# First token block with gate, value and last output pair in three float32r products, weight splits staged through device memory, and one written-out order

## The chip, the cores and the metric

The kernel runs on one core of one Trainium2 chip. The metric is device time of one execution in microseconds (us), lower is better. The engines named below are TensorE (PE in the profile; PEld is its weight load), VectorE (DVE), ScalarE (ACT), GpSimd (POOL) and SyncE (SP). SP and POOL do no arithmetic here that matters; they issue the DMAs, each in its own program order.

## The reference

Attention without a softmax over scores, then a gated feed-forward layer, all in float32:

```python
def _attn_ref(q, k, v):                      # batch 8, heads 8, seq 576, head_dim 64
    q_s = softmax(q, axis=-1)                # max, exp, sum + 1e-09
    k_s = softmax(k, axis=2)
    kv = np.einsum('bhsd,bhse->bhde', k_s, v)
    return np.einsum('bhsd,bhde->bhse', q_s, kv)

def _moe_ref(x, w_gate, w_val, w_out):       # 4608 tokens, d_model 512, d_ff 1536
    gate = 1.0 / (1.0 + np.exp(-(x @ w_gate)))
    val = x @ w_val
    return gate * val @ w_out
```

`x` is the attention output, tokens by 512 features. The float32 weights come to the chip as pairs of 32-bit words (float64 bits) and are narrowed there.

## The kernel before

The 4608 tokens go in nine token blocks of 512 (`w` = 0 to 8; the change calls a block a span). The 1536 hidden columns go in twelve slices `j` of 128, or six pairs `p` of two slices. For each block the kernel makes `x` (512 features by 512 tokens), then hidden activations by two products (gate and value), a sigmoid, a product, and the output product.

Blocks 1 to 8 work in split float32r: each operand is a high part (float32 rounded to float32r) plus a low part (the rest), and a product is three matmuls, high by high, high by low, low by high, each with 256 columns. Gate and value of a pair are done by a seven-product scheme (`g1`, matmuls on L770) on a 2x2 blocking: three weight blocks A11, A12, A22 stay in memory on the core for good as high and low parts (`a_w`), and four sums of weight blocks, S1 to S4, go through one buffer `s_sb`, which is loaded again for each pair from device memory (`s_load`, L311, 512 KB each). The output product (`g2`, L856) takes `wo_hl`, high and low parts of the output weights, also loaded for each pair (`wo_load`, L261).

Token block 0 is different. It runs while the weights arrive, and its products are plain float32 matmuls of 512 columns: `g1_0` (L718) for gate and value, `g2_0` (L752) for the output, one slice `j` at a time. Each plain float32 matmul stands in the trace as two records. Beside it, in the same 130 us, the weights are prepared for the later blocks: narrowed (`w_low`, `w_top`, `w_join`, the same for `wo`), summed (`w_sums`, into the buffer `four`), split (`split_hi` on ACT L294, `split_lo` on DVE L299; `wo_hi` on ACT L244, `wo_save` on DVE L248), and the high and low parts of the sums and of the output weights are stored to device memory by POOL (L304, L251). The attention part of block 1 runs there too.

Token block 1 goes through the pairs in the order 5, 0, 1, 2, 3, 4, so that the pair split last comes first. The finished block 0 leaves through `acc_out`: four ACT copies from the accumulators into `x_32` (L744), then four DMAs from `x_32` (L745, issued by SP).

The order of work is the order of the calls in the code: on each engine the instructions run in that order, each waiting for what it needs. Where the transposed row maxima of the next block's queries are needed (`qn_send`, `q_spread`), SP sends them to device memory and reads them back spread over partitions (L517, L559), for the maxima and later for the reciprocals. Three PSUM buffers `gv` serve all gate and value products; `y` and `z` of a pair are copied out by ACT (L793 to L812) between products that add to them.

```python
def g1_0(j):            # block 0: 2 x 4 plain float32 matmuls of 512 columns
    nc.tensor.matmul(ps[n], lhsT=w[:, kt // 2, sl], rhs=x_0[:, kt], ...)
```

Of the kernel before, what the change touches and what calls it, by code (L numbers as in the profile page):

```python
# [8 lines left out]
F32 = mybir.dt.float32  # L9
# [8 lines left out]
P = 128  # L18
# [32 lines left out]

@with_exitstack
def attn_moe(ctx: ExitStack, tc: tile.TileContext, qf, qn, qT, k, kT, v, wgv, wo, out):
# [34 lines left out]
    f_last = const.tile([P, 4, 2, 2 * P], F32, name="f_last")  # L88
    s_dram = [spool.tile([P, 4 * 4 * 2 * P], F32, name=f"s_{p}") for p in range(NS)]
# [116 lines left out]
    def w_on_vector(j):  # L206
        return j == 1

    def w_low(j):
        narrow_low(w_raw[j])  # L210
        if w_on_vector(j):
            narrow_sign_bits(w_raw[j])

    def w_top(j):
        if not w_on_vector(j):
            narrow_sign(w_raw[j])
        narrow_abs(w_raw[j], w_both(j))

    def w_join(j):
        narrow_join(w_raw[j], w_both(j))  # L220

    def wo_on_vector(j):
        return j % 2 and j > 6

    def wo_low(j):
        narrow_low(wo_raw[j])
        if wo_on_vector(j):
            narrow_sign_bits(wo_raw[j])

    def wo_top(j):  # L230
        if j % 2 == 0:
            wo_t[j // 2] = wpool.tile([P, 2, DM], F32, name="wo_t")
        if not wo_on_vector(j):
            narrow_sign(wo_raw[j])
        narrow_abs(wo_raw[j], wo_t[j // 2][:, j % 2])
# [28 lines left out]

    s_32 = {}

    def w_sums(p):

        f = f_w[p].rearrange("p b n e -> p b (n e)")
        s_32[p] = t = four  # L270

        def tt(o, x, y, op):
            nc.vector.tensor_tensor(out=t[:, o], in0=x, in1=y, op=op)

        tt(S1, f[:, 2], f[:, 3], ALU.add)
        tt(S2, t[:, S1], f[:, 0], ALU.subtract)
        tt(S3, f[:, 0], f[:, 2], ALU.subtract)
        tt(S4, f[:, 1], t[:, S2], ALU.subtract)

    def split_of(p):  # L280
        f = f_w[p].rearrange("p b n e -> p b (n e)")
        s = s_sb.rearrange("p s h n e -> p s h (n e)")
        a = a_w[p].rearrange("p b h n e -> p b h (n e)")
        return [(a[:, A11:A12 + 1], f[:, 0:2])] + [
            (s[:, i:i + 2], s_32[p][:, i:i + 2]) for i in (0, 2)
        ] + [(a[:, A22:A22 + 1], f[:, 3:4])]

    def split_hi(p, parts=range(4)):

        if p not in a_w:  # L290
            a_w[p] = apool.tile([P, 3, 2, 2, 2 * P], F32R, name="a_w", tag=f"a{p}")
        for i in parts:
            o, x = split_of(p)[i]
            nc.scalar.copy(out=o[:, :, 0], in_=x)  # L294

    def split_lo(p, parts=range(4)):
        for i in parts:
            o, x = split_of(p)[i]
            nc.vector.tensor_tensor(  # L299
                out=o[:, :, 1], in0=x, in1=o[:, :, 0].bitcast(F32), op=ALU.subtract  # L300
            )
            if 1 <= i <= 2:
                n = 8 * 2 * P
# [1038 lines left out]
```

## Time and profile before

| | |
|---|---|
| Device time, median of 3 runs | 926.0 us (924.47 to 926.96) |
| Profiled execution, from its first to its last instruction | 925.1 us |
| PE busy | 917.0 us, 99% |
| DVE busy | 604.7 us, 65% |
| ACT busy | 478.6 us, 52% |
| POOL busy | 168.2 us, 18% |
| DMA, mean over the span | 278 GB/s |
| Granted PE clock | 1.00 |

The page gives no other time for the profiled execution than its span; it lies inside the spread of the three timed runs, 0.9 us below their median. PE is busy nearly all the time, so what PE has to do, and the few places where it stands still, make the time. The share of DVE and ACT is an average: both are far busier while block 0 runs than later.

### The profile page before, as it was taken

How to read it: one execution, taken by the hardware profiler on the slowest of the kernel's cores; microseconds unless marked ns; L12 is line 12 of the kernel's file. 1: busy time of each engine (PE TensorE's matmuls, PEld its weight loads, DVE VectorE, ACT ScalarE, POOL GpSimd, SP SyncE). 2: the span in 40 equal slices, each digit the busy share in tenths (PEclk: the TensorE clock that was granted, in tenths of full speed). 3: DMA queues.
4: the chain of work that ended last, by engine and by line, in shares of the span. 5: the costliest groups of instructions: out<-in, count | busy, mean ns of one | idle time of the engine just before them, and what ended most of it. 6: DMA issues, size and time to landing. Idle time of an engine off the chain costs nothing.

```text
span 925.1 us, 18593 instructions
## 1 busy us (share of the span) xinstructions
PE 917.0 (99%) x7556; PEld 835.5 (90%) x7556; DVE 604.7 (65%) x973; ACT 478.6 (52%) x800; POOL 168.2 (18%) x320
## 2 busy tenths in 40 slices
PE   9999999998999999999999999999999999999998
PEld 6445545898999999999999999999999999999998
DVE  7998979846766577656766666666746574664242
ACT  3879986735455455644663456354725443543222
POOL 0010101221121212122121122112221122212220
PEclk9999999999999999999999999999999999999999
DMA  9995776999899999999999899999997799768772
GB/s 311 390 398 194 288 254 252 361 336 319 214 311 330 323 247 264 325 325 289 236 326 326 285 246 302 323 289 251 304 302 209 224 262 324 232 187 257 214 208 69
DMA packets 93268, 256.93 MB, mean 278 GB/s; under 512 B 15160, under 2 KB 17728, under 8 KB 90240
## 3 DMA queue, kind: packets, MB, share of 16 engines
q0 software_dynamic: 44288, 167.27, 60.4%
q1 hardware_dynamic: 48896, 88.47, 32.4%
q8 instruction: 60, 0.98, 0.4%
q14 instruction: 24, 0.20, 0.1%
HBM read 227.15 MB, written 28.56 MB: 276 GB/s over the span
## 4 chain that ended last, share of the span: by engine, by line
PE 91%; DMA 5%; DVE 1%; SPq 1%; ACT 1%; issue 0%; DVEq 0%
PE gv L770 46%; PE acc L856 27%; PE gv L718 9%; PE acc L752 4%; PE gv L637 2%; PE at L440 2%; DMA four<-q_m_row 2%; DMA out<-x 1%; DMA ring<-qT_in 1%; PE at L637 1%; DMA wo_raw<-wo_in 1%; SPq L396 1%; DMA lent<-k_in 1%; PE acc L658 0%; DVE q_m L525 0%
## 5 line engine op out<-in xcount | busy, mean ns | idle before, releaser
L770 PE MATMUL gv<-c_hl,s_sb 128*128 128x256 f32 x2304 | 277.4, 276 | 2.9 <-ACT sg L802 2.7
L770 PEld LDWEIGHTS gv<-c_hl,s_sb 128*128 128x128 f32 x2304 | 268.7, 188 | 3.5 <-ACT sg L802 3.1
L856 PE MATMUL acc<-wo_hl,h 128*128 128x256 f32 x2304 | 269.4, 276 | 0.0
L856 PEld LDWEIGHTS acc<-wo_hl,h 128*128 128x128 f32 x2304 | 264.6, 188 | 0.4
L770 PE MATMUL gv<-c_hl,a_w 128*128 128x256 f32 x1728 | 220.2, 277 | 0.0
L770 PEld LDWEIGHTS gv<-c_hl,a_w 128*128 128x128 f32 x1728 | 206.9, 188 | 1.0 <-issue 0.7
L311 POOL DMA_DIRECT2D s_sb<-s x188 | 101.3, 539 | 308.5 <-PE gv L770 303.2
L789 DVE TENSOR_TENSOR sg<-gv,sg 128x512 f32<-128x512 f32 x48 | 33.2, 691 | 152.5 <-PE gv L770 152.5
L261 POOL DMA_DIRECT2D wo_hl<-wo x94 | 50.7, 539 | 280.1 <-PE acc L856 280.1
L802 ACT COPY sg<-gv 128x512 f32<-128x512 f32 x48 | 28.2, 587 | 131.4 <-PE gv L770 121.7
L812 ACT COPY sg<-gv 128x512 f32<-128x512 f32 x48 | 28.2, 587 | 99.8 <-PE gv L770 99.8
L814 DVE TENSOR_TENSOR sg<-sg 128x512 f32<-128x512 f32 x48 | 33.2, 692 | 56.8 <-ACT sg L812 56.8
L718 PE MATMUL gv<-x,f_w 128*128 128x512 f32 x160 | 70.2, 593 | 0.0
L718 PEld LDWEIGHTS gv<-x,f_w 128*128 128x128 f32 x160 | 30.0, 190 | 36.3 <-issue 34.2
L835 DVE TENSOR_TENSOR h<-sg,h 128x1024 fp32r<-128x1024 f32 x48 | 58.8, 1226 | 1.6
L817 ACT ACTIVATE sg<-sg 128x512 f32<-128x512 f32 x48 | 30.4, 634 | 50.3 <-DVE sg L816 50.3
L823 DVE TENSOR_TENSOR sg<-sg 128x512 f32<-128x512 f32 x48 | 33.2, 692 | 33.6 <-ACT sg L817 33.6
L798 ACT COPY sg<-gv 128x512 f32<-128x512 f32 x48 | 28.2, 587 | 40.3 <-PE gv L770 40.3
L793 ACT COPY sg<-gv 128x512 f32<-128x512 f32 x48 | 28.2, 587 | 36.2 <-PE gv L770 36.2
L752 PE MATMUL acc<-wo_t,h 128*128 128x512 f32 x96 | 43.2, 592 | 0.0
L752 PEld LDWEIGHTS acc<-wo_t,h 128*128 128x128 f32 x96 | 18.2, 190 | 22.5 <-issue 21.8
L816 DVE TENSOR_TENSOR sg<-gv,sg 128x512 f32<-128x512 f32 x48 | 33.2, 691 | 2.7 <-PE gv L770 0.5
(162 smaller groups left out, 993.6 us busy)
## 6 DMA issues: line engine op xcount, KB each, us to landing
s_sb<-s POOLq DMA_DIRECT2D x188, 512.0 KB, 7.3
wo_hl<-wo POOLq DMA_DIRECT2D x94, 512.0 KB, 6.1
s<-s_sb POOLq DMA_DIRECT2D x12, 1024.0 KB, 6.6
out<-x SPq DMA_DIRECT2D x35, 256.0 KB, 5.5
ring<-k_in SPq DMA_DIRECT2D x28, 256.0 KB, 6.0
ring<-qn_in SPq DMA_DIRECT2D x28, 256.0 KB, 4.8
four<-q_m_row SPq DMA_DIRECT2D x56, 128.0 KB, 12.0
ring<-qT_in SPq DMA_DIRECT2D x28, 256.0 KB, 10.4
```

Of the source, the lines that this page charges most:

```text
L261: nc.gpsimd.dma_start(out=t.rearrange("p h e -> p (h e)"), in_=wo_dram[2 * p + i].bitcast(F32R))
L311: nc.gpsimd.dma_start(out=s_sb[:, i].rearrange("p h n e -> p (h n e)"), in_=s_dram[p][:, i * n:(i + 1) * n].bitcast(F32R),)
L718: nc.tensor.matmul(ps[n], lhsT=w[:, kt // 2, sl], rhs=x_0[:, kt], start=(kt == 0), stop=(kt == NK - 1),)
L752: nc.tensor.matmul(acc[0][m], lhsT=h_0[j][:, m * P:(m + 1) * P], rhs=wo_t[j // 2][:, j % 2], start=(j == 0), stop=(j == NJ - 1),)
L770: nc.tensor.matmul(ps[:, n], lhsT=lh(kt), rhs=c_hl[i][:, x, kt], start=(first and n == 0 and kt == 0 and lh is wh and x == 0), stop=(last ...
L789: nc.vector.tensor_tensor(out=sg[:, 0], in0=rr, in1=sg[:, 0], op=ALU.add)
L814: nc.vector.tensor_tensor(out=sg[:, 3], in0=sg[:, 3], in1=sg[:, 2], op=ALU.add)
L816: nc.vector.tensor_tensor(out=sg[:, 1], in0=z, in1=sg[:, 1], op=ALU.add)
L817: nc.scalar.activation(sg[:, 0:2, 0], sg[:, 0:2, 0], AF.Sigmoid)
L823: tt(out=sg[:, 0:2, 0], in0=sg[:, 0:2, 0], in1=sg[:, 0:2, 1], op=ALU.mult)
L835: nc.vector.tensor_tensor(out=lo, in0=sg[:, :, 0], in1=hi.bitcast(F32), op=ALU.subtract)
L856: nc.tensor.matmul(acc[w][m][:, es], lhsT=h[lh][:, i, sl], rhs=o[i][:, rh, es], start=(at == 0 and i == 0 and lh == 0 and rh == 0 and e == 0),
```

## The change

Block 0 takes split operands for gate and value. Its `x` is split on the way out of the accumulators (`x_hi` on ACT, `x_lo` on DVE), and slices `j` are multiplied as three products from the high and low parts of A11, A12, A22 and, new, A21, whose parts lie in half of `s_sb` for the time. The output product stays plain float32 for slices 0 to 9 and is split for 10 and 11.

The sums S1 to S4 and the output weights of pairs 0 to 4 are no longer split in block 0. They are stored as float32 (`s_save`, `wo_save`; 1 MB and 512 KB a pair), and in block 1, pair by pair, read back into a staging buffer (`s_in` into the four slots of `x_32`, `wo_in` into part of `f_last`, 256 KB each), split there (`s_hi`, `wo_hi` on ACT; `s_lo`, `wo_lo` on DVE) into `s_sb` and `wo_hl`, used, and stored as high and low parts (`s_store`, `wo_store`, 512 KB each) for blocks 2 to 8. Block 1 so loads no high and low parts.

From the first instruction to the end of block 1, one written list of some 1,000 words gives the order (`ORDER`, played by `go`); blocks 2 to 8 keep their loops.

```diff
+ORDER = """
+k0_in.0 warm.16 k0_in.2 k0_in.4 warm.2 q0_in.0.2 q0_in.2.2 k_own.0 v_load.0.3 load_w.0 k_top.1
...
+g2_0.10 c_hi.6 g_mul_0.11 s_in.0.2 g1_s2.5 s_hi.0.1 h_hi_0.11 g1_s1.5 s_lo.0.1 h_lo_0.11
...
-    def wo_save(j):
-        t = wo_out[j]
-        nc.vector.tensor_tensor(
-            out=t[:, 1], in0=wo_t[j // 2][:, j % 2], in1=t[:, 0].bitcast(F32), op=ALU.subtract
-        )
-        nc.gpsimd.dma_start(out=wo_dram[j], in_=t.rearrange("p h e -> p (h e)").bitcast(F32))
+    def wo_save(p):
+        nc.gpsimd.dma_start(out=wo32_dram[p], in_=wo_t[p].rearrange("p h e -> p (h e)"))
...
+    def s_save(p):
+        t = four
+        if p < NS - 1:
+            nc.gpsimd.dma_start(
+                out=s32_dram[p], in_=t.rearrange("p s e -> p (s e)")
+            )
...
+        if j % 2 == 0:
+            return [(a_w[p][:, A11:A12 + 1], f[:, 0:2])]
+        if p not in t21:
+            t21[p] = s_sb[:, p % 2:p % 2 + 1]
+        return [(t21[p], f[:, 2:3]), (a_w[p][:, A22:A22 + 1], f[:, 3:4])]
...
+    def stage(i):
+        return x_32[:, i] if i < 4 else f_last[:, 3].rearrange("p n e -> p (n e)")
...
+    def s_in(p, i, eng=nc.sync):
+        n = 2 * 2 * P
+        eng.dma_start(out=stage(i), in_=s32_dram[p][:, i * n:(i + 1) * n])
+
+    def s_hi(p, i):
+        nc.scalar.copy(out=s_sb[:, i, 0].rearrange("p n e -> p (n e)"), in_=s_src(p, i))
+
+    def s_lo(p, i):
+        hi, lo = (s_sb[:, i, h].rearrange("p n e -> p (n e)") for h in range(2))
+        nc.vector.tensor_tensor(out=lo, in0=s_src(p, i), in1=hi.bitcast(F32), op=ALU.subtract)
+
+    def s_store(p, i):
+        n = 4 * 2 * P
+        nc.gpsimd.dma_start(
+            out=s_dram[p][:, i * n:(i + 1) * n],
+            in_=s_sb[:, i].rearrange("p h n e -> p (h n e)").bitcast(F32),
+        )
...
     def x_ev_0(hp):
         ps = x_ps.pop((0, hp))
-        if hp % 2:
-            nc.vector.tensor_copy(out=x_0[:, hp], in_=ps)
-        else:
-            nc.scalar.copy(out=x_0[:, hp], in_=ps)
+        hi = x_hi[hp // 2][:, hp % 2]
+        nc.scalar.copy(out=hi, in_=ps)
+        nc.vector.tensor_tensor(
+            out=x_lo[:, hp], in0=ps, in1=hi.bitcast(F32), op=ALU.subtract
+        )
...
+    def g1_0(j, n):
+        ps = ps_gv.tile([P, T], F32, name="gv")
+        gate.setdefault(j, {})[n] = ps
+        blocks = [o[:, i] for o, _ in split_of(j) for i in range(o.shape[1])]
+        parts = [(0, 0), (0, 1), (1, 0)]
+        if j == 0 and n == 0:
+            parts.insert(1, parts.pop())
+        for at, (lh, lo) in enumerate(parts):
             for kt in range(NK):
-                sl = slice((kt % 2) * P, (kt % 2 + 1) * P)
-                nc.tensor.matmul(
-                    ps[n], lhsT=w[:, kt // 2, sl], rhs=x_0[:, kt],
-                    start=(kt == 0), stop=(kt == NK - 1),
-                )
-        gate[j] = ps
+                w = blocks[kt // 2][:, lh, n, (kt % 2) * P:(kt % 2 + 1) * P]
+                x = x_lo[:, kt] if lo else x_hi[kt // 2][:, kt % 2]
+                for e in range(2):
+                    es = slice(e * HT, (e + 1) * HT)
+                    nc.tensor.matmul(
+                        ps[:, es], lhsT=w, rhs=x[:, es],
...
+            for lh, rh in ((0, 0), (0, 1), (1, 0)):
+                for e in range(2):
+                    es = slice(e * HT, (e + 1) * HT)
+                    nc.tensor.matmul(
+                        acc[0][m][:, es], lhsT=h_r[j][:, lh, sl], rhs=wo_hl[1, NS - 1][j % 2][:, rh, es],
...
+    def g1_s1(p):
+        prod(y_z["z"], wsum(S1), T1, True, False)
+        nc.scalar.copy(out=sg[:, 2], in_=y_z["z"])
...
+    def go(order):
+        for word in order.split():
+            name, *args = word.split(".")
+            ops[name](*(int(x) if x.isdigit() else x for x in args))
```

Three places of the new order follow. The first is DVE in the head, between the running maximum of the first keys and the reduction of its transpose. Before, one query maximum (L525) stands ahead of that reduction (L1137):

```order
L1127 TENSOR_TENSOR lent<-lent 64x512
L525 TENSOR_REDUCE q_m<-lent 128x8
L1137 TENSOR_REDUCE kmax_237<-acc 128x4
L1140 TENSOR_TENSOR lent<-ident,kmax_237 128x512
L525 TENSOR_REDUCE q_m<-lent 128x8 x3
L532 TENSOR_TENSOR lent<-lent,q_m 128x512 x4
```

Now four maxima (L694) and three subtractions (L701) stand ahead of it (L1295):

```order
L1286 TENSOR_TENSOR lent<-lent 64x512
L694 TENSOR_REDUCE q_m<-lent 128x8 x3
L701 TENSOR_TENSOR lent<-lent,q_m 128x512
L694 TENSOR_REDUCE q_m<-lent 128x8
L701 TENSOR_TENSOR lent<-lent,q_m 128x512 x2
L1295 TENSOR_REDUCE kmax_249<-acc 128x4
L1298 TENSOR_TENSOR lent<-ident,kmax_249 128x512
```

Three maxima and three subtractions have moved ahead of the reduction.

The second is ACT where block 0 leaves its accumulators in block 1. Before, the four copies into `x_32` (L744) are followed by the four copies-out of the next pair's products (L802, L798, L793, L812):

```order
L744 COPY x_109<-acc 128x512 x4
L802 COPY sg<-gv 128x512
L798 COPY sg<-gv 128x512
L793 COPY sg<-gv 128x512
L812 COPY sg<-gv 128x512
```

Now (L944, then L995, L1007, L1003, L1011 for the same copies-out) the splits of the staged sums (L430 `s_hi`, reading `x_109`, which is `x_32`) and of the staged output weights (L357 `wo_hi`) stand between them:

```order
L944 COPY x_109<-acc 128x512 x4
L521 ACT_TABLE_LOAD
L521 ACTIVATE kt_116,k_sum<-kt_116,k_neg 128x576
L995 COPY sg<-gv 128x512
L1007 COPY sg<-gv 128x512
L521 ACTIVATE kt_115,k_sum<-kt_115,k_neg 128x576
L430 CAST s_sb<-x_109 128x512
L1003 COPY sg<-gv 128x512
L430 CAST s_sb<-x_109 128x512
L582 ACTIVATE ring<-ring 128x512
L1011 COPY sg<-gv 128x512
L357 CAST wo_hl<-f_last 128x512
```

The first L430 of that stretch is `s_hi` of pair 1 for S2; it stands ahead of the copy-out L1003 of pair 0.

The third is SP at the same place. Before, the four output DMAs (L745) are followed by two key loads and the spread maxima:

```order
L517 DMA q_m_row_1204<-q_m_1199 128x32
L745 DMA out_0<-x_32_109 128x512 x4
L331 DMA kt_0_115<-kT_in 128x576
L331 DMA kt_1_116<-kT_in 128x576
L559 DMA four_111<-q_m_row_1204 64x512 x8
```

Now the reads of the staged sums of pair 1 (L427, into the slots of `x_32` from which the output leaves) follow the output DMAs (L945), and those of pair 2 the spread maxima (L728):

```order
L945 DMA out_0<-x_32_109 128x512 x4
L427 DMA x_32_109<-s32_1_120 128x512 x3
L496 DMA kt_1_116<-kT_in 128x576
L427 DMA x_32_109<-s32_1_120 128x512
L496 DMA kt_0_115<-kT_in 128x576
L735 DMA ring_1831<-qT_in 128x512
L686 DMA q_m_row_1836<-q_m_1614 128x32
L728 DMA four_111<-q_m_row_1836 64x512 x4
L427 DMA x_32_109<-s32_2_121 128x512
```

A read into a slot of `x_32` waits until the output DMA from that slot has landed.

## Rows read from the trace of the kernel before

**Rows 1.** The page: span, PE, and granted clock in 40 slices
```profile
span 925.1 us, 18593 instructions
PE 917.0 (99%) x7556; PEld 835.5 (90%) x7556; DVE 604.7 (65%) x973; ACT 478.6 (52%) x800; POOL 168.2 (18%) x320
...
PEclk9999999999999999999999999999999999999999
```

**Rows 2.** Chain of waits in order of time: start us, us, what
```profile
27.09 13.73 PE gv L718 x32
...
44.37 6.87 PE gv L718 x16
51.23 3.43 PE acc L752 x8
...
174.32 11.54 DMA out<-x
...
248.71 5.44 PE acc L856 x48
254.15 9.52 PE gv L770 x84
```

**Rows 3.** Stretches of the span: us, busy and instructions by engine, clock, DMA
```profile
27.09:155.84 128.75, 128.75 (x404) 60.89 (x404) 113.61 (x170) 110.22 (x137) 12.83 (x24) 1.00 0.78 293
155.84:254.15 98.31, 95.37 (x859) 92.65 (x858) 67.24 (x112) 48.99 (x90) 21.11 (x40) 1.00 1.06 307
20.00:70.00 50.00, 49.91 (x156) 23.48 (x152) 46.38 (x72) 38.65 (x45) 3.89 (x7) 1.00 1.02 394
...
160.00:235.00 75.00, 72.06 (x660) 69.34 (x659) 49.03 (x84) 39.42 (x71) 16.55 (x31) 1.00 1.12 332
```

**Rows 4.** Waits from 155 to 240: engine, waited for, total us, times, longest
```profile
PE gv L770 <- ACT sg L802: 2.7, 1, 2.7
```

**Rows 5.** DVE in order of time, in the head: start us, us, what
```profile
8.93 0.67 DVE L525 TENSOR_REDUCE q_m<-lent 128x8 f32<-128x512 f32 x1
10.79 0.69 DVE L1137 TENSOR_REDUCE kmax<-acc 128x4 f32<-128x512 f32 x1 [1.19 <-PE acc L1131]
...
12.20 1.86 DVE L525 TENSOR_REDUCE q_m<-lent 128x8 f32<-128x512 f32 x3
13.98 2.49 DVE L532 TENSOR_TENSOR lent<-lent,q_m 128x512 f32<-128x512 f32 x4
...
21.45 0.86 DVE L454 TENSOR_TENSOR f_last<-acc,k_r 64x256 f32<-64x256 f32 x2
```

**Rows 6.** DVE in order of time, in block 0
```profile
47.96 1.22 DVE L186 SCALAR_TENSOR_TENSOR f_w<-f_w,x 128x1024 int32<-128x1024 int32 x1
49.09 0.68 DVE L186 SCALAR_TENSOR_TENSOR wo_t<-wo_t,wo_raw 128x512 int32<-128x512 int32 x1
49.70 0.69 DVE L164 TENSOR_SCALAR w_raw<-w_raw 128x1024 uint32<-128x1024 uint32 x1
50.30 0.42 DVE L164 TENSOR_SCALAR wo_raw<-wo_raw 128x512 uint32<-128x512 uint32 x1
```

**Rows 7.** Groups from 0 to 240: count, busy us, mean ns, idle before
```profile
L299 DVE TENSOR_TENSOR s_sb<-four,s_sb 128x1024 fp32r<-128x1024 f32 x12 | 14.2, 1217 | 0.0
...
L248 DVE TENSOR_TENSOR wo_hl<-wo_t,wo_hl 128x512 fp32r<-128x512 f32 x12 | 8.2, 683 | 0.0
```

**Rows 8.** DMA issues from 160 to 235: count, KB each, median us to landing
```profile
s_sb<-s POOLq DMA_DIRECT2D x20, 512.0 KB, 8.7
...
out<-x SPq DMA_DIRECT2D x4, 256.0 KB, 11.0
...
ring<-qT_in SPq DMA_DIRECT2D x4, 256.0 KB, 9.3
```

**Rows 9.** DMA issues of the whole span, as in rows 8
```profile
out<-x SPq DMA_DIRECT2D x35, 256.0 KB, 5.5
...
ring<-qn_in SPq DMA_DIRECT2D x28, 256.0 KB, 4.8
```

More of the change, by code (lines that the diff above doesn't have):

```diff
@@ L204, in w_both, with w_sign @@
         return w_tile(j).rearrange("p b n e -> p (b n e)")
[L206 to L207 removed]
     def w_low(j):
         narrow_low(w_raw[j])
[L211 to L223, printed above, removed]
+    def w_sign(j):
+        narrow_sign(w_raw[j])
@@ L265, in attn_moe, with w_sum @@
     s_32 = {}
-    def w_sums(p):
+    def w_sum(p, o):
         f = f_w[p].rearrange("p b n e -> p b (n e)")
         s_32[p] = t = four
[L272 to L286, printed above, removed]
@@ L288, in split_hi @@
-    def split_hi(p, parts=range(4)):
+        x, y, op = {
+            S1: (f[:, 2], f[:, 3], ALU.add), S2: (t[:, S1], f[:, 0], ALU.subtract),
+            S3: (f[:, 0], f[:, 2], ALU.subtract), S4: (f[:, 1], t[:, S2], ALU.subtract),
+        }[o]
+        nc.vector.tensor_tensor(out=t[:, o], in0=x, in1=y, op=op)
+    def s_save(p):
[4 more added lines that the diff above has]
+            )
+    t21 = {}
@@ L290, in split_hi, with split_of @@
+    def split_of(j):
+        p = j // 2
+        f = f_w[p]
         if p not in a_w:
             a_w[p] = apool.tile([P, 3, 2, 2, 2 * P], F32R, name="a_w", tag=f"a{p}")
[L292 to L298, printed above, removed]
+        if j % 2 == 0:
[3 more added lines that the diff above has]
+        return [(t21[p], f[:, 2:3]), (a_w[p][:, A22:A22 + 1], f[:, 3:4])]
@@ new lines, in d_part, with d_split, d_store, sd_hi @@
+    def d_part(i):
+        return (s_sb[:, 2 + i % 2, h].rearrange("p n e -> p (n e)") for h in range(2))
+    def d_split(i, x):
+        hi, lo = d_part(i)
+        nc.vector.tensor_tensor(out=lo, in0=x, in1=hi.bitcast(F32), op=ALU.subtract)
+    def d_store(i, to):
+        nc.gpsimd.dma_start(
+            out=to, in_=s_sb[:, 2 + i % 2].rearrange("p h n e -> p (h n e)").bitcast(F32)
+        )
+    def sd_hi(p, i):
+        nc.scalar.copy(out=next(d_part(i)), in_=four[:, i])
+    def sd_lo(p, i):
+        d_split(i, four[:, i])
@@ L309, in s_load, with sd_store, od_hi, od_lo @@
+    def sd_store(p, i):
+        n = 4 * 2 * P
+        d_store(i, s_dram[p][:, i * n:(i + 1) * n])
+    def od_hi(j):
+        nc.scalar.copy(out=next(d_part(j)), in_=wo_f32(j))
+    def od_lo(j):
+        d_split(j, wo_f32(j))
+    def od_store(j):
+        d_store(j, wo_dram[j])
     def s_load(p, i):
@@ new lines, in attn_moe, with prod @@
+    y_z = {}
+    def prod(ps, ws, i, first, last):
+        for n in range(2):
+            wh, wl = ws(n)
+            for kt in range(2):
+                for lh, x in ((wh, 0), (wh, 1), (wl, 0)):
+                    nc.tensor.matmul(
+                        ps[:, n], lhsT=lh(kt), rhs=c_hl[i][:, x, kt],
+                        start=(first and n == 0 and kt == 0 and lh is wh and x == 0),
+                        stop=(last and n == 1 and kt == 1 and lh is wl),
+                        skip_group_check=True,
+                    )
@@ new lines, in wa, with wsum, g1_a11, g1_a12 @@
+    def wa(p, i):
+        a = a_w[p]
+        return lambda n: [lambda kt, h=h: a[:, i, h, n, kt * P:(kt + 1) * P] for h in range(2)]
+    def wsum(i):
+        return lambda n: [lambda kt, h=h: s_sb[:, i, h, n, kt * P:(kt + 1) * P] for h in range(2)]
+    def g1_a11(p):
+        y_z["y"], y_z["z"], y_z["r"] = (ps_gv.tile([P, 2, HT], F32, name="gv") for _ in range(3))
+        prod(y_z["y"], wa(p, A11), B11, True, False)
+        nc.scalar.copy(out=sg[:, 0], in_=y_z["y"])
+    def g1_a12(p):
+        prod(y_z["r"], wa(p, A12), B21, True, True)
+        nc.vector.tensor_tensor(out=sg[:, 0], in0=y_z["r"], in1=sg[:, 0], op=ALU.add)
@@ L861, in g2 @@
                     )
-        if at == NS - 1:
+        if at == NS - 1 and 1 in parts:
             acc_out(w)
@@ L946, in load_next @@
         if p == 2 and b is not None:
-            if not first:
-                for t in vs:
-                    v_load(b, t)
+            for t in range(5):
+                v_load(b, t)
             k_max(b, 0); k_max(b, 1)
```

688 lines of the change are left out of this document (320 added, 368 removed).

## The prediction

> **What bounds the kernel now.** I read the page first: PE is busy 99% of the span and its granted clock is full in every slice [rows 1]. So time can come from only two places: PE work that goes, and PE standing still. Next, the chain of waits in order of time: from 27.09 us it runs nearly without a break through PE, first L718 (gate and value of token block 0) and L752 (its output product), then the split products [rows 2]. The stretches give the size of the standing: from 27.09 to 155.84 (block 0) PE is busy 128.75 of 128.75 us, and from there to 254.15, where block 2 begins, 95.37 of 98.31 [rows 3]. PE thus stands still for 2.94 us in block 1, and 2.7 of these are one wait for an ACT copy-out [rows 4]. From 254.15 on the changed kernel does what the kernel did before, so I forecast when block 2 begins and leave the rest at its 671 us. The same stretches show how close the other engines are: in block 0 DVE is busy 113.61 of 128.75 us, ACT 110.22; in block 1 it is 67.24 and 48.99 of 98.31 [rows 3].
>
> **PE work removed.** Gate and value of one slice take 16 records of L718, 6.87 us [rows 2]. Afterwards they are 2 halves x 3 products x 4 x 2 = 48 matmuls of 256 columns in float32r. The output product of the later blocks is just 48 such matmuls on the same shapes, in 5.44 us [rows 2]. Twelve slices save 12 x (6.87 - 5.44) = 17.2 us. Output slices 10 and 11 go from 3.43 us each to 24 matmuls, 5.44 / 2 = 2.72: 1.4 us. Together 18.6 us. If PE also stopped standing still, 2.9 more: 21.5 us is the most that the change can give, and block 2 would begin at 232.6.
>
> **What it costs in the head.** DVE now runs four query maxima and three subtractions, instead of one maximum, ahead of the reduction L1137. Before, this started at 10.79, just when the transposes were there. One maximum takes 0.67, further ones 0.60 (1.86 for three) and a subtraction 0.6 (2.49 for four) [rows 5]: from 8.93 on that is 4 x 0.62 + 3 x 0.6 = 4.3, so the reduction starts near 13.2, 2.4 later. What follows, to the key-value result L454 at 21.45, also gets one narrowing more ahead of it. And the last of the four `x` parts to be split on ACT is the first that the new products need. I take 2.7 us; ends 0 (the keys' exponentials on PE and ACT remain the pacemaker) and 4 (none of it overlaps).
>
> **Block 0 on DVE.** DVE loses the low parts of ten of the twelve sum pieces, 10 x 1.22 = 12.2 us, and of ten output slices, 6.8 us [rows 7]. It gains the low parts of A21, six of 0.6, two more for `x`, and sign extractions that ACT did. Issue to issue, a 1024-wide operation takes 1.13 us (47.96 to 49.09), a 512-wide one 0.61 (49.09 to 49.70) and a short shift 0.33 from start to next start [rows 6]; by these the new list holds 103 us of DVE work between the first product of block 0 and the first of block 1. PE has there 12 x 5.44 + 10 x 3.43 + 8.2 of attention = 108 us. That is nearly level, where it was 113.6 to 128.8. One spot is tighter: from the first product to the second half of slice 4, PE has nine halves and two output slices, 9 x 2.72 + 2 x 3.43 = 31.3 us, and DVE, starting 2 us later, 30.0 us up to the multiplication that frees the PSUM buffer which that half needs. I take 2 us of waiting for it all. Ends: 0.5, and 8, if DVE loses here to its own waits what it lost before, which the slack in its busy time then hid.
>
> **The first pair change in block 1.** The order of DMAs, ACT and PE closes a loop here that did not exist. The staged S2 of pair 1 goes into the slot of `x_32` from which block 0 leaves. So: PE ends the last output slice; ACT copies; the output DMA lands; only then is the staged read issued; it lands; `s_hi` runs; and behind `s_hi` in ACT's order stands the copy-out of S1's product of pair 0, for which the product S4 on PE waits. From the end of the second accumulator to S4, PE has 1.4 us of output product and four products of 12 matmuls (5.44 us), 6.8 in all; the chain has about 2 us of ACT and issue plus two landings. The standing is therefore both landings less 4.8 us. Output DMAs landed after 11.0 us here, and SP's read of a quarter megabyte after 9.3 [rows 8]; that would be 15.5 us. Over the whole run the same two kinds take 5.5 and 4.8 [rows 9]; that would be 5.5. The first pair of figures was measured with some 3 MB of POOL's loads in flight; these are replaced by stores of pair 0, 2.1 MB, which at 394 GB/s [rows 3] drain in 5.3 us, most of it before the output starts, and while PE stands no further stores come. I take 7.5 + 6.0, hence 8.7 us. This is the largest unknown.
>
> The Trainium skill, "DMA: Bandwidth & Descriptors", section "Where 436 GB/s comes from", says that the HBM side, about 358 GB/s for one core, binds transfers between HBM and SBUF. The row of 20 to 70 us shows a mean of 394 GB/s [rows 3], so the trace disagrees. From the first product of block 1 to the first of its third pair 12.1 MB are asked for against 27 us of PE; by the page's figure that is an estimated 33.8 us, 6.8 of waiting, and by the row's rate 30.7 us, 3.7 of waiting, both inside the wait just priced. The sum goes by the landings.
>
> **The rest of block 1.** DVE gains 30 low parts, 18.3 us at 0.61, on 67.24 busy of 98.31; ACT 30 high parts, some 16 us on 48.99. Both stay under 90% of the stretch, hidden beside PE as long as the data is there. DMA: each of 30 pieces now moves 256 KB in and 512 KB out in place of 512 KB in, 7.9 MB more; the 25 MB of 160 to 235 (332 GB/s for 75 us [rows 3]) become some 33 MB in 93 us, 353 GB/s, still under 394. What this does to the spread of the query maxima, which SP now issues between staged reads, no row shows; I take 2.5 us, ends 0 and 10.
>
> **Sum.** -21.5 + 2.7 + 2.0 + 8.7 + 2.5 = -5.6 us. The profiled execution would go from 925.1 to 919.5; it lies 0.9 below the median of the runs shown, so the median goes from 926.0 to 920.4.
>
> **The rivals.** *Little waiting (A).* Both landings at the light values, head and block 0 at their low ends, no other wait: -21.5 + 5.5 to 7 gives about -15, 911; with no standing at all 905. For it: the loads that made the landings long are gone. Against: in the same place the output DMA is on the chain with 11.54 us [rows 2].
>
> *The gain turns into waiting (B).* DVE paces block 0 (8 in place of 2) or the landings are near 11 and 9: between -2.8 and +2.8, 926. For it: DVE at 103 of 108 us. Against: it lags the products it feeds by a few us of slack in most places.
>
> *Slower (C).* SP is one queue in order, and the staged reads of pairs 2 to 4 stand behind spread reads that wait for their own sends. If a staged read comes late in each of five pair changes, every change stands like the first: 15.5 once and about 3 in the four others, 27.5 with head and block 0 at 4.7: -21.5 + 32.2 = +10.7, 937. It decides once the waits in block 1 exceed 17 us. For it: the first loop's measured landings alone make 15.5. Against: a pair takes 15 us of PE (9.5 + 5.44), a landing 9 to 11.
>
> The Trainium skill, "TensorE: Matmul & The Clock Gate", section "What's actually happening", says that an idle PE falls to 1.2 GHz until it has been busy again. In this trace the clock stays at 1.00 with PE idle for 2.7 us at one time; no run shows a longer gap. It would add to C and to the upper part of the forecast.
>
> **How the numbers follow.** The forecast (waits between its ends, 912 to 923) has a chance of 0.44, A 0.22, B 0.16, C 0.18. About 0.3% (2.8 us) is what a measurement of this kernel tells from no change. Forecast and A are faster by more: 0.66; B is no change: 0.16; C slower: 0.18. The range reaches from A's 907, without its fastest part, up to 930, which takes in the lighter half of C; the forecast's own is 912 to 923.
>
> **What would show it.** Records of the gate and value products of block 0 should come in groups of 48 in 5.44 us. The first of them should start near 30 instead of 27.09. In block 0 PE should have gaps of a few us in total, ended by DVE. One gap of 5 to 15 us should stand in block 1 ahead of the fourth sum's product of pair 0, with an output DMA and a staged read one behind the other on the chain. Block 2 should begin near 248.5, and what follows last 671 us. The forecast is wrong if that gap is missing (A), if later pair changes stand as long (C), or if PE waits for DVE through block 0 (B).

## The result, and the profile after

The changed kernel takes 933.54 us (median of 4 runs, 931.79 to 934.83) against 925.24 (4 runs, 923.15 to 926.96): a ratio of 1.0094, 95% interval 1.0072 to 1.0117. It is 8 us slower, where 920.4 had been forecast, and outside the range of 907 to 930.

The profiled execution spans 933.0 us. Cut at the starts of block 0, block 1, block 2 and at a point in block 2 from which both kernels run alike, it has these stretches (start and end; us, then busy time and instructions of PE, PEld, DVE, ACT and POOL, granted clock, DMA share, GB/s):

```profile
28.77:144.07 115.30, 112.79 (x780) 92.23 (x781) 106.04 (x166) 89.25 (x119) 8.87 (x16) 0.99 0.76 275
144.07:256.82 112.75, 103.68 (x899) 101.83 (x898) 79.64 (x135) 72.06 (x127) 25.88 (x48) 0.97 0.90 311
256.82:304.40 47.58, 45.26 (x429) 44.80 (x428) 28.64 (x48) 24.47 (x43) 9.71 (x18) 0.96 1.08 293
304.40:933.00 628.60, 624.95 (x5701) 623.18 (x5700) 373.90 (x611) 284.89 (x515) 123.98 (x230) 1.00 0.92 265
```

The same two stretches at the end of the kernel before:

```profile
254.15:296.21 42.06, 42.06 (x429) 41.80 (x428) 28.03 (x47) 24.47 (x42) 9.17 (x17) 1.00 1.11 321
296.21:925.10 628.89, 624.96 (x5701) 623.18 (x5700) 373.74 (x611) 284.96 (x515) 123.99 (x230) 1.00 0.93 265
```

Block 0 is shorter by 13.4 us (115.30 against 128.75 in [rows 3]), block 1 is longer by 14.4 (112.75 against 98.31, though it now holds two output slices of block 0 and held one before), and the start of block 2, which does the same work, is longer by 5.5. The last stretch is the same in both. The clock tells more: 1.00 everywhere before [rows 1, 3], now below it in three stretches.

A stand is in what follows a stretch in which PE does nothing once block 0 has begun, and a fall is a stretch at the lower clock. The waits of PE in the first 300 us of the changed kernel (what it waited for: total us, times, longest):

```profile
PE gv L978 <- ACT sg L995: 5.2, 3, 2.4
PE gv L978 <- ACT sg L1011: 4.0, 2, 3.3
PE gv L752 <- issue: 1.9, 1, 1.9
...
PE gv L903 <- ACT x_hi L835: 1.7, 1, 1.7
PE gv L978 <- ACT sg L1007: 1.6, 2, 0.8
```

Before, block 1 had one such line, of 2.7 us [rows 4], and a wait of 0.2 us. No single wait is large. From the first product of block 0 on, PE stands 2.5 us in block 0, 9.1 in block 1 and 2.3 in block 2: 13.9 us. The clock after the four longest of these stands, in the changed kernel:

```profile
99.73:103.14 3.41, 3.41 (x17) 3.41 (x17) 3.29 (x7) 1.46 (x4) 0.00 (x0) 0.50 0.97 370
164.70:168.10 3.40, 3.40 (x18) 3.40 (x18) 0.00 (x0) 1.62 (x4) 0.00 (x0) 0.52 0.86 284
229.45:232.85 3.40, 3.40 (x18) 3.40 (x17) 3.40 (x7) 2.94 (x6) 1.30 (x3) 0.50 1.02 416
294.30:297.70 3.40, 3.40 (x18) 3.40 (x17) 0.08 (x1) 0.58 (x1) 0.55 (x1) 0.50 1.29 281
```

Each time PE is busy all through, at 1.2 in place of 2.4 GHz. Half of 3.4 us of PE's work is lost: 1.7 us four times, 6.8 us. The stands ahead of them were 1.9, 2.4, 3.3 and 2.3 us long.

Such a loss is not always a loss of the whole. Here is the same work of block 0, from the end of its first stand to the end of its last, in the changed kernel and in e3_next_queries, an experiment below in which the clock stayed up there (columns as above):

```profile
99.60:108.04 8.44, 7.87 (x53) 7.58 (x53) 7.91 (x14) 6.49 (x11) 0.00 (x0) 0.80 0.69 266
99.80:108.25 8.45, 6.38 (x52) 5.99 (x52) 7.91 (x14) 6.55 (x11) 0.00 (x0) 1.00 0.70 262
```

Both take the same time, with DVE busy 7.91 us: at the full clock PE waits 1.5 us for DVE in between, and at the lower one it does not. So the first fall took no time: without it, other stands would have.

The third thing is the pace of the products at full clock. Two output products of the changed kernel, 48 products of 256 columns each, in the timeline of PE (start us, us, instruction):

```profile
195.91 5.60 PE L1092 MATMUL acc<-wo_hl,h 128*128 128x256 f32 x48
...
251.00 5.82 PE L1092 MATMUL acc<-wo_hl,h 128*128 128x256 f32 x48
```

They differ by 0.22 us, at a clock of 1.00 in both; from start to start it is 113.3 against 117.8 ns per product. Counted from the starts of the records, 1202 products of the changed kernel come 115.5 to 121 ns after the one before, against 166 in the kernel before: 1036 x 4.5 ns = 4.7 us. Most of the slower stretches do not begin at a stand. The first begins after the first plain float32 output product (L954), where PE did not stand at all (eight products of the same shapes before and after it; start us, us):

```profile
32.52 1.07 PE L903 MATMUL gv<-x_lo,a_w 128*128 128x256 f32 x8
...
37.05 3.59 PE L954 MATMUL acc<-wo_t,h 128*128 128x512 f32 x8
...
44.25 1.10 PE L903 MATMUL gv<-x_lo,a_w 128*128 128x256 f32 x8
```

The longest, of 410 products from 242.6 to 293.6, begins behind six small products (L806). Only some 65 of the slower products stand in stretches that began at a stand, those of 0.6 us near 108 and 3.3 us near 229.

Why PE stood in block 1 is read from the chain of waits (start us, us, what):

```profile
193.81 0.56 POOL f_last L351
...
194.42 9.26 DMA x<-s
203.76 0.62 ACT s_sb L430
...
205.12 0.59 ACT sg L1007
...
218.28 9.48 DMA x<-s
227.86 0.09 ACT s_sb L430
...
228.39 0.59 ACT sg L1011
...
266.17 11.11 DMA ring<-qn_in
```

These two staged reads land 9.3 and 9.5 us after their issue, ACT waits for them in its order, and the copy-out that PE needs stands behind. Not all are so late; the sixteen reads of staged sums between 150 and 230 us:

```profile
DMA to landing us min/median/max: 3.0/6.3/12.0
```

In block 2 the next queries come the same way: SP issued their last read only at 266.17.

### The profile page after: what moved, and what is told of

Its sections match the earlier page's. It is cut to its first block, busy times and chain, and to the rows that moved or that the text cites. A ratio compares the mean times of both kernels' runs of the same rounds, so it can differ in the third digit from the quotient of the medians.

```text
span 933.0 us, 19514 instructions
## 1 busy us (share of the span) xinstructions
PE 910.9 (98%) x7972; PEld 877.5 (94%) x7972; DVE 614.4 (66%) x998; ACT 484.4 (52%) x826; POOL 169.5 (18%) x322
## 4 chain that ended last, share of the span: by engine, by line
PE 84%; DMA 6%; DVE 4%; ACT 4%; issue 1%; SPq 1%; POOL 0%; DVEq 0%; POOLq 0%; ACTq 0%
PE gv L978 46%; PE acc L1092 26%; PE gv L903 4%; DMA x<-s 2%; PE acc L954 2%; PE gv L806 2%; PE at L609 1%; DMA ring<-qn_in 1%; DMA s<-four 1%; PE at L806 1%; DVE q_m L694 1%; DMA f_last<-wo 0%; DMA lent<-k_in 0%; DMA kmax_row<-kmax_b 0%; ACT wo_raw L262 0%
## 5 line engine op out<-in xcount | busy, mean ns | idle before, releaser
L978 PE MATMUL gv<-c_hl,s_sb 128*128 128x256 f32 x2304 | 280.9, 278 | 7.4 <-ACT sg L995 5.2
L978 PEld LDWEIGHTS gv<-c_hl,s_sb 128*128 128x128 f32 x2304 | 271.8, 189 | 8.6 <-ACT sg L995 5.8
L978 PEld LDWEIGHTS gv<-c_hl,a_w 128*128 128x128 f32 x1728 | 209.3, 190 | 4.8 <-ACT sg L1011 4.4
L476 POOL DMA_DIRECT2D s_sb<-s x168 | 90.6, 539 | 282.1 <-PE gv L978 281.0
L346 POOL DMA_DIRECT2D wo_hl<-wo x84 | 45.3, 539 | 255.3 <-PE acc L1092 255.3
L995 ACT COPY sg<-gv 128x512 f32<-128x512 f32 x48 | 28.1, 585 | 121.9 <-PE gv L978 118.9
L1011 ACT COPY sg<-gv 128x512 f32<-128x512 f32 x48 | 28.1, 586 | 95.7 <-PE gv L978 95.7
L1007 ACT COPY sg<-gv 128x512 f32<-128x512 f32 x48 | 28.2, 587 | 39.2 <-PE gv L978 39.1
L1003 ACT COPY sg<-gv 128x512 f32<-128x512 f32 x48 | 28.1, 586 | 31.9 <-PE gv L978 31.8
L903 PE MATMUL gv<-x_hi,a_w 128*128 128x256 f32 x288 | 41.8, 286 | 1.7 <-ACT x_hi L835 1.7
L903 PEld LDWEIGHTS gv<-x_hi,a_w 128*128 128x128 f32 x288 | 37.6, 193 | 3.1 <-ACT x_hi L835 2.5
L954 PE MATMUL acc<-wo_t,h 128*128 128x512 f32 x80 | 35.3, 592 | 0.0
L1063 DVE CAST h<-sg 128x1024 fp32r<-128x1024 f32 x44 | 30.5, 693 | 1.3
```

What stands on the lines that cost most here:

```text
L346: nc.gpsimd.dma_start(out=t.rearrange("p h e -> p (h e)"), in_=wo_dram[2 * p + i].bitcast(F32R))
L476: nc.gpsimd.dma_start(out=s_sb[:, i].rearrange("p h n e -> p (h n e)"), in_=s_dram[p][:, i * n:(i + 1) * n].bitcast(F32R),)
L903: nc.tensor.matmul(ps[:, es], lhsT=w, rhs=x[:, es], start=(at == 0 and kt == 0 and e == 0), stop=(at == 2 and kt == NK - 1 and e == 1), sk ...
L954: nc.tensor.matmul(acc[0][m], lhsT=h_0[j][:, sl], rhs=wo_f32(j), start=(j == 0), stop=False, skip_group_check=True,)
L978: nc.tensor.matmul(ps[:, n], lhsT=lh(kt), rhs=c_hl[i][:, x, kt], start=(first and n == 0 and kt == 0 and lh is wh and x == 0), stop=(last ...
L1063: copy(out=h_part(w, p, 0), in_=sg[:, :, 0])
```

## Experiments

Ratios are to the kernel before, run on the same chip.

**Again.** 

> The changed kernel once more, for comparison on the same chip as the next three. Expected 933.5 us with a spread of 1.5, PE standing at the same four places (1.9 us near 98, 2.4 near 161, 3.3 near 226, 2.3 near 291), each followed by about 3.4 us at a granted clock of 0.50. If the stands were chance, their places would differ in this profile.

Measured 932.96 us, 1.0080 (1.0062 to 1.0098). PE stood at the same places (2.4 us near 98, 2.5 near 162, 2.6 near 224, 2.1 near 288), but the clock fell after only two of them, near 98 and 224. So the stands belong to the program; what follows one differs between executions.

**The first change of pair.** The edit, in the written order:

```
- ... s_in.1.2 k_sum.2.3 qn_max.2.3 ... g1_a11.0 g1_s2.0 k_sum.2.2
+ ... s_in.1.2 qn_max.2.3 ... g1_a11.0 k_sum.2.3 g1_s2.0 k_sum.2.2
```

> On ACT the table load and the first exponential of the keys go behind the copy-out L995 of pair 0, which they delayed from 160.8 to 162.8. Theory (the loop of the prediction exists and is covered by this stand): the 2.4 us stand near 161 shrinks to under 0.6, and a new one of about 3 us opens ahead of the product S4 of pair 0, because its copy-out L1003 stands behind s_hi, whose staged read landed at 167.8 whatever PE does; time 932 to 934, no gain. Rival (the order on ACT alone is the cost): no new stand, 2 us of standing and 1.7 us of lower clock go, 929.5.

Measured 933.46 us, 1.0089 (1.0070 to 1.0108): no gain, as the theory had it. PE in this kernel's timeline:

```profile
165.06 4.37 PE L978 MATMUL gv<-c_hl,s_sb 128*128 128x256 f32 x36 [1.53 <-ACT sg L995]
171.39 1.65 PE L978 MATMUL gv<-c_hl,s_sb 128*128 128x256 f32 x12 [1.96 <-ACT sg L1003]
```

The loop of the prediction is there: a stand of 1.96 us ahead of S4 for the copy-out behind `s_hi`. In the changed kernel the earlier stand covers it. The earlier stand kept 1.5 us where under 0.6 was named, and the new one has 2.0 instead of about 3.

Then the splits of pair 1 as well:

```
- s_hi.1.1 g1_s1.0 s_hi.1.0 s_lo.1.1 s_lo.1.0 qn_sub.2.3 ... g1_s3.0 g1_s4.0
+ g1_s1.0 g1_s3.0 g1_s4.0 s_hi.1.1 s_hi.1.0 s_lo.1.1 s_lo.1.0 qn_sub.2.3 ...
```

> As e1_exp_later, and s_hi and s_lo of pair 1 for S2 and S1 also go behind the copies-out L1003 and L1011 of pair 0, so that nothing on ACT that PE needs waits for the staged read. Theory: both stands at the first pair change are gone, 2.4 us of standing and 1.7 us of lower clock: 929.4. Rival (the staged data is late for everything): the splits of pair 1 come later and PE stands at the start of pair 1 instead; 932 or more.

Measured 933.33 us, 1.0086 (1.0067 to 1.0104). The stand ahead of S4 was gone and that near 161 down to 1.0 us, but one of 3.15 us opened at 181, at the start of pair 1. The rival held.

**Block 0.** `s_save.2` goes ahead of `k_max_rows.1`.

> In POOL's order the store of the float32 sums of pair 2 (L386) goes ahead of the two key-maximum DMAs (L536, L541), the second of which waits for the landing of the first. The buffer four then comes free some 4 us earlier for the sums of pair 3, for which DVE waited until 85.4. Theory (block 0 stands because of this one store): DVE gains 3 to 5 us, the stands of 1.9 and 0.6 us near 98 and 107 go and with them 3.4 us at the half clock: 929.3. Rival (DVE is simply full in block 0, and any spare time is lost to its next wait): the stand moves on or shrinks by under 1 us; 932.5 or more.

Measured 931.57 us, 1.0074 (1.0052 to 1.0096). The waits of DVE in block 0, of the changed kernel:

```profile
DVE four L381 <- DMA s<-four: 3.2, 1, 3.2
...
DVE ring L572 <- DMA kmax_b<-kmax_row: 1.6, 1, 1.6
```

and of this one:

```profile
DVE ring L572 <- DMA kmax_b<-kmax_row: 4.6, 1, 4.6
```

DVE waited 4.8 us for two DMAs, one behind the other on POOL; with the order turned round it waits 4.6 for the other. The theory fell: the stand near 98 still had 1.7 us. The time lies between what theory and rival named, 929.3 and 932.5.

**SP's order.** Three kernels: `k_max_read.3` behind `qn_load.3.0`; `s_in.4.1` ahead of `wo_in.3.0`; both.

> In SP's order at the end of block 1 the read of the key maxima (L541), which waits 11 us for its own send, goes behind the last read of the next queries (L680). That read was issued at 266.2 and landed 11.1 us later, and PE stood 2.3 us near 291 for the copy-out behind the exponentials made from it. Theory (the queue's order made it late): it is issued near 254 instead, the stand goes, and 1.7 us of lower clock in the runs that had it there; 2.3 to 4 us less, 929 to 931. Rival (ACT's work there is the bound, not the data): the stand stays above 1.5 us, time within 1 us of 933.

> In SP's order the staged read of the sum S2 of pair 4 goes ahead of one read of staged output weights, two spread reads and a value read: issued near 207 instead of 218.3. ACT waited 5.2 us for it and PE 3.3 us, near 226. Theory (SP's order): the read lands by 217, the stand goes, and where the clock fell behind it another 1.7 us: 928 to 930. Rival (the DMA engines are full there, and what is read earlier makes something else later): a stand of 2 us or more at the same pair change, ended by another staged read or by the spread reciprocals; 932 or more.

> The SP moves of e3_next_queries and e4_staged_early together. Alone, the first took away the stand near 288 and left 3.3 us near 224; the second took away the one near 224 and left 6.0 us near 288. If the stands have separate causes, both go: about 5.6 us of standing and up to 3.4 us of lower clock less than 933, 925 to 928. If a full DMA engine passes the wait on to whatever is read next, stands of 3 us or more open elsewhere in block 1 or 2: 931 or more.

The first took 931.25 us, 1.0081 (1.0062 to 1.0101): the stand in block 2 was gone, that near 224 stayed at 3.3. The second took 933.29, 1.0095 (1.0060 to 1.0131): the stand near 224 fell to 0.4, but in block 2 PE stood for 6.0 us, up to 293.30. The last read of the next queries and the copy-out made possible by it, from the chain of this kernel:

```profile
267.51 10.02 DMA ring<-qn_in
...
292.78 0.48 ACT sg L995
```

In the changed kernel the queries landed at 277.3 (266.17 and 11.11, above) and the stand ended at 293.06. So nothing came later here: PE reached this place 3.4 us earlier and lost what it had gained, in front of data that came when it came before. Both moves together took 929.31, 1.0044 (1.0028 to 1.0059), 4 us less, between the two forecasts. The two stands have separate causes, one behind the other, and the second hides what is gained at the first.

**The load of the stores.**

> Leaves out the 30 stores of high and low parts of pairs 0 to 4 in block 1 (512 KB each, 15.7 MB); later blocks load the parts of pair 5 in their place, so their values differ and their DMAs do not. Theory (the DMA load of block 1 makes the staged reads late): reads that took 9 us land in 5, PE stands in block 1 for the ACT order alone (2.4 us instead of 9.1), and SP is earlier for block 2 (2.3 us and the lower clock less there too): 922 to 926. Rival (the order of issue alone makes them late): 9 us of standing in block 1 stay within 2 us; 931 or more.

> Leaves out the 30 staged reads (7.9 MB); the splits work on what the staging buffers hold, so the values of the sums and of the output weights of pairs 0 to 4 are wrong, and all stores stay. Theory and rival agree that every stand tied to a staged read goes (5 to 6 us between 180 and 232, and the stand in block 2 since SP has 20 issues less); what is left is the stand near 161 behind ACT's exponentials (2.4 us) and block 0's 2.5: 921 to 926. If the stands stay, they are not from staging at all, and both are wrong.

> All 30 stores of block 1 stay in their places and keep their waits, but move 64 of 1024 columns each (32 KB instead of 512 KB; later blocks load pair 5's parts, so values differ). The kernel without the stores took 921.8 us; it took away the load on the DMA engines and also freed POOL's order, where staged reads stand behind stores. Theory (the load of 15.7 MB is the cost): as without the stores, 920 to 924, the staged reads on POOL landing in about 5 us instead of 9.4. Rival (POOL's order is the cost): staged reads still wait behind the stores, 929 or more.

Without the stores 921.80 us, 0.9969 (0.9957 to 0.9982); without the staged reads 924.22, 1.0002 (0.9985 to 1.0018); with small stores in their places 923.15, 0.9980 (0.9968 to 0.9991). Block 1 of the first and the last (columns as above):

```profile
143.33:244.25 100.92, 98.22 (x899) 97.36 (x897) 79.39 (x135) 71.57 (x127) 10.34 (x19) 1.00 0.63 198
```

```profile
144.09:245.36 101.27, 98.21 (x898) 97.35 (x897) 79.37 (x135) 71.70 (x127) 26.00 (x48) 1.00 0.65 207
```

Either way block 1 takes 101 instead of 112.75 us, with a stand of 2.0 or 2.4 us near 161 and one of 0.7. The small stores keep every place in POOL's order and every wait, so it is enough to take away their bytes. Staged reads issued by POOL, in the changed kernel, then with small stores (count, KB each, median us to landing):

```profile
x<-s POOLq DMA_DIRECT2D x6, 256.0 KB, 9.4
```

```profile
x<-s POOLq DMA_DIRECT2D x6, 256.0 KB, 5.4
```

**Orders together.**

> All staged reads of the sums of pairs 2 to 4, and of the output weights after the first, are issued by POOL, each directly ahead of the store that waits for the same split; none is left behind SP's spread reads. The bytes are the same. Theory (load, and the order among the DMAs): reads go ahead of the stores that compete with them and are issued up to 10 us earlier, so the stands of 3.3 us near 226 and of 2.3 us near 291 go and those near 202 to 212 shrink: 926 to 929. Rival (the load alone, whatever the order): 931 or more.

> As f5_reads_on_pool, with the ACT order of e2_split_behind, the SP move of e3_next_queries, and in block 0 the store of the sums of pair 2 ahead of the key-maximum DMAs together with the four subtractions of these maxima behind the sums of pair 3 on DVE. If every stand comes from an order: block 0 loses 2 to 3 us of its 3.5 us of stands, the change of pair near 161 its 2.4, and the clock stays up: 916 to 922, faster than both kernels. If the DMA load and a full DVE are behind them: 928 or more, with stands at other places.

> The changed kernel with the two SP moves of f3_both_moves and the block 0 order of f4_all_moves, staged reads and ACT order as they were. f3_both_moves took 929.3. Theory (what is left is the load of the stores and a full DVE): block 0 gains under 1.5 us, and stands of 2 us or more stay in block 1: 927 to 930, still slower than before. Rival (orders alone are to blame): 924 or less.

Reads on POOL: 935.30 us, 1.0109 (1.0085 to 1.0133), on the rival's side. The reads of the sums that POOL issued landed after 5.7 us (median of twelve) instead of 9.4 (of six) although all bytes still moved, at 312 GB/s in the mean; so the place among the stores counts beside their bytes. Yet PE still stood 3.0 and 2.9 us at two places in block 1 and 2.9 in block 2. The second of them, near 202, was for a read of output weights, from the chain of this kernel:

```profile
193.98 9.36 DMA f_last<-wo
```

POOL had issued two stores of 512 KB just ahead of it, and ACT waited for it in front of the copy-out that PE needed. All moves: 928.49, 1.0039 (1.0023 to 1.0054), in the upper of the two ranges. The three orders: 926.00, 1.0013 (0.9997 to 1.0028), as fast as the kernel before, and between what theory and rival named: block 0's first stand fell from 1.9 to 0.4 us and the clock stayed up there (which by the rows above gains nothing more), block 2 kept only 0.7, and 2.4 and 2.0 stayed in block 1, each with a fall. Its edit in block 0, beside the moves of SP:

```
- k_max_rows.1 kv_hi.0 s_save.2 ... k_sub.1.0 k_sub.1.1 ... k_sub.1.3 ... k_sub.1.4 ... k_exp.1.1 ... w_sum.3.2 qn_sub.1.3 qn_sum.1.2 ...
+ s_save.2 k_max_rows.1 kv_hi.0 ... w_sum.3.2 qn_sub.1.3 qn_sum.1.2 k_sub.1.1 k_sub.1.0 k_sub.1.3 k_sub.1.4 ... k_exp.1.1 ...
```

> f6_three_orders (926.0) and, further: h_hi of pair 0 on ACT and h_lo on DVE go ahead of the exponentials and the split of staged output weights that stood before them (0.3 us stand near 184, 3.1 in e2_split_behind); wo_hi of pair 2 goes behind the copies-out of pair 2, so that ACT no longer waits 6.1 us for its staged read in front of them (2.0 us near 201); the product L918 of slice 7 goes ahead of the key sums on DVE (1.5 us near 102); and the ACT order of e2_split_behind (2.4 us near 160). Theory (a stand costs its length and, behind the longer ones, 1.7 us of lower clock): 5 to 6 us of standing and the two falls of the clock that f6 still had, 3.4 us, go: 917 to 921, faster than both kernels. Rival (under the load of the stores each wait moves to the next thing read): 924 or more.

> f7_stands_removed without the ACT order of e2_split_behind, so that the stand of 2.4 us near 160 stays. By the first theory it takes 2 to 4 us more than f7, 920 to 924; by the rival the two are alike within 1 us, since pair 1's splits come later in f7.

Measured 926.67 us, 1.0029 (1.0012 to 1.0046), and 926.25, 1.0017 (1.0000 to 1.0034): nothing more was gained, and neither median was under 924. The stands moved: near 105 PE stood 2.65 us for ACT (`h`, L914) in place of 1.5 and 0.6 for DVE and ACT, near 203 for 1.5 and 2.6 us for L1007 instead of 2.0 for L995. The rival held. No version found beats the kernel before with all its work done.

**Stands put into the kernel before.** In blocks 2 to 8, for some pairs:

```
-        nc.scalar.copy(out=sg[:, 0], in_=y)
+        for _ in range(1 + MORE.get((w, p), 0)): nc.scalar.copy(out=sg[:, 0], in_=y)
```

> The kernel before, unchanged in what it computes, with 14 stands of PE put into blocks 2 to 8 where it otherwise runs without a break: the copy-out of the first product of a pair is made 3 to 11 times instead of once (0.48 us each on ACT), and the next product into the same buffer waits. Stands of about 0.2 to 4.0 us, 26 us in all. Theory (a stand of PE brings the lower clock and can leave PE in the slower of its two paces, 117.8 ns instead of 113.3 per product of 256 columns): every stand over 2.9 us is followed by 3.4 us or more at 0.50, those of 1.5 to 2.9 some of the time, shorter ones never; and some stretches after a stand run at 117.8 until the next; 925 + 26 + 7 to 12 for the clock + up to 12 for the pace. Rival (both come from the work in blocks 0 and 1, not from the stands): clock 1.00 and 113.3 throughout, 951.

> The same with 21 stands, in each of blocks 2 to 8 one of about 1.6, one of 2.6 and one of 0.7 us, 34 us in all. Theory: some of the stands of 2.6 and few of 1.6 are followed by the lower clock, at 1.7 us each, and the pace changes at some of them either way; 925 + 34 + 5 to 25. Rival: 959 with no lower clock and no change of pace.

Measured 985.05 us (2 runs, 981.87 and 988.23) and 1007.46 (1001.30 and 1013.63); the profiled spans are 986.5 and 999.5. The stands came out longer than meant, 0.55 to 5.5 us, so both spans lie above the 975 and 984 us to which the theory's sums go. In the second kernel, from its timeline of PE:

```profile
650.23 5.60 PE L856 MATMUL acc<-wo_hl,h 128*128 128x256 f32 x48
...
663.17 1.68 PE L770 MATMUL gv<-c_hl,s_sb 128*128 128x256 f32 x12 [1.17 <-ACT sg L802]
...
670.34 5.82 PE L856 MATMUL acc<-wo_hl,h 128*128 128x256 f32 x48
...
685.89 5.82 PE L856 MATMUL acc<-wo_hl,h 128*128 128x256 f32 x48
...
696.88 1.93 PE L770 MATMUL gv<-c_hl,s_sb 128*128 128x256 f32 x12 [2.35 <-ACT sg L802]
```

The same instruction on the same shapes takes 5.60 us ahead of a stand of 1.17, and 5.82 after it; apart from two falls, the slower pace lasted to 729.7, behind the small products of L440. And the clock of the same kernel, after a stand of 2.41 us that ended at 272.48 and after two of 3.64:

```profile
273.00:276.40 3.40, 3.40 (x32) 3.40 (x32) 0.69 (x1) 0.59 (x1) 0.54 (x1) 1.00 1.09 361
291.90:295.30 3.40, 3.40 (x18) 3.40 (x17) 0.00 (x0) 0.59 (x1) 0.54 (x1) 0.50 0.71 265
397.70:401.10 3.40, 3.40 (x19) 3.40 (x18) 0.00 (x0) 0.59 (x1) 0.54 (x1) 0.50 0.89 297
```

Of the 35 inserted stands of both kernels, none of the 11 from 0.55 to 1.73 us was followed by the lower clock, 5 of the 10 of 2.35 to 2.41 were, 1 of the 3 of 3.02, and all 11 of 3.58 to 5.49. "Every stand over 2.9" was thus too much by two. The first kernel's 61.4 us over the kernel before are 37.5 of stands (40.2 in the row of L802, less 2.7 of before), 14.3 of clock (half of the 28.5 us in which PE worked at 0.50) and 7.4 of pace (1673 more products at 4.45 ns): 59.2. The second's 74.4 are 47.7, 17.0 and 5.0: 69.7. The rest was not broken down. So stands alone, in work that otherwise runs at full clock and pace, bring both. The rival fell.

## Why the prediction was wrong, step by step

**The work removed.** 18.6 us were forecast, at 5.44 us per 48 products. That row [rows 2] stands in a stretch at the faster pace; in block 0 most slices took 5.66, as here in the chain of the changed kernel:

```profile
124.84 5.66 PE gv L903 x48
```

Twelve slices at that price save 14.5 us instead of 17.2. This part of the loss needs no stand.

**The head.** Forecast 2.7, measured 1.7: the first product came at 28.77.

**Block 0.** 2.0 us of standing forecast, 2.5 measured. The longer stand, up to 99.60, ended with a step of DVE as said, the shorter one, of 0.6, with ACT:

```profile
98.81 0.69 DVE L744 TENSOR_TENSOR ring<-ring,q_r 128x512 f32<-128x512 f32 x1
```

DVE was busy 106.0 of 115.3 us.

**The first change of pair.** 8.7 us forecast ahead of S4. Wrong in place and size: the stand was 2.4 us, three products earlier, ahead of S2. The chain names what ended it, the copy-out of the first product, behind ACT's copies of the accumulators and a table load and exponential:

```profile
162.07 0.87 ACT kt L521 x2
162.94 0.48 ACT sg L995
```

The loop exists (e1_exp_later) but is worth some 2 us: the output DMAs landed after 3.3 us (median of four), and the staged read, issued by 164.4, was there at 167.8, where landings of 7.5 and 6.0 had been taken from between [rows 8] and [rows 9]. By the forecast's own sign the missing gap meant A, 911; the time went the other way, since the other terms grew.

**The rest of block 1.** 2.5 us forecast; the stands there, after the first, come to 6.6. This was rival C's mechanism, staged reads late at the later changes of pair: without the reads (e7_no_staged_reads) only 0.7 of the 6.6 stays. With the first change C had priced it at 27.5 us, and it came to 9.1. I had called 353 GB/s "still under 394"; the reads took 9 us to land while the stretch moved 311. The mean rate of a stretch did not say how long a read takes behind stores: 9.4 us at 311 GB/s, 5.7 at 312 with the reads on POOL, 5.4 at 207 with small stores. By the Trainium skill, "DMA: Bandwidth & Descriptors", section "Where 436 GB/s comes from", a transfer between HBM and SBUF is bound near 358 GB/s. The traces disagree: 394 over 50 us in [rows 3], and 416 over 3.4 us in one of the rows on the clock above.

**Block 2 on.** Left at its 671 us; it took 676.2, by 2.3 of standing, 1.7 of clock and a slower pace up to the stand that ended at 293.06 (some 290 products, 1.3 us).

**The step that failed.** All stands forecast come to 2.0 + 8.7 + 2.5 = 13.2 us, all measured ones to 13.9. With head and stands as measured, and every stand priced at its length, the sum is 925.1 - 18.6 - 2.9 + 1.7 + 13.9 = 919.2 us, against 919.5 forecast. The span was 933.0. The 13.8 us between are the lower clock, 6.8, and the slower pace and the rest, 7.0, of which the count above gives 4.7; the other 2.3 were not broken down. So the places were mostly wrong, their total right by luck, and two prices failed. The larger is that of a stand: I took it to be its length, where the falls behind four of them took 6.8 us more of PE's time. The lower clock was named, as an addition to rival C, and given no time because the one stand before, of 2.7 us, had kept the clock at 1.00. The Trainium skill, "TensorE: Matmul & The Clock Gate", section "What's actually happening", has the rule that an idle PE falls to 1.2 GHz until it is busy again. The traces agree that falls come behind stands, and differ in that only some stands have one; a single stand without a fall was no ground to leave it out. The smaller is that of a product: I took it from a stretch at the faster pace, where 1161 products between 28.77 and 304.40 ran at the slower one, against 125 between 27.09 and 296.21 before.

**The range.** The ends that the forecast gives for its waits add up to 6.0 and 37.5 us (0 to 4, 0.5 to 8, 5.5 to 15.5, 0 to 10), which is 910.5 to 942; the 912 to 923 that it calls its own is narrower without a reason given, and the measured time lies inside the sum of its ends.

Shown by runs: that block 1 is 11 us shorter and the staged reads come earlier once the bytes of the stores are gone (e6_no_stores, f1_tiny_stores), that orders alone give back 6 to 7 us with all bytes moved (f6_three_orders), and that stands bring the lower clock and can change the pace (both p kernels). Not settled: what decides whether a given stand does, what the two paces are, and what begins the slower one where PE has not stood. Not tried: storing part of the splits in block 2 instead of block 1.

## What to carry to other kernels

Where TensorE runs without a break, a new break may cost more than its length: price a stand at its length plus, for those of about 2 us or more, up to the 1.7 us that a fall took here, and nothing where PE would wait for another engine right after. Do not take a product's price from an unbroken stretch for a broken one. Before moving traffic to just ahead of its use, look at landing times under the stores that the change adds, not at the mean rate. Where an in-order queue is full, removing one named wait mostly shows the next: take the load away once (small transfers in the same places) before spending edits on the order.

## What was not expected

Products of 256 columns at granted clock 1.00 have two paces, 113.3 and 117.8 ns, each kept for up to hundreds of products. A stand can turn either into the other, and so can plain float32 products or a few small products between, with no stand at all. Plain float32 products of 512 columns (two records, 0.86 us) showed one pace in both kernels, 6.87 us per sixteen records in [rows 2] and, from 112.47, in the chain of the changed kernel. The fall near 100 us cost no time in any kernel: the work between these two stands took 8.42 to 8.46 us in five traces with a fall there and in nine without. And one execution of the kernel with inserted stands fell to 0.50 after the 1.84 us stand that the kernel before has at that place, where the profile of before shows 1.00 after 2.7.
